# One PSUM bank for cosine and sine products, and the cosine product in three one-pass products

## The chip, the cores and the metric

The kernel runs on one core of one Trainium2 chip. The metric is device time in microseconds, the median of the runs. The core's engines are TensorE (PE in the profile, its weight loads PEld), VectorE (DVE), ScalarE (ACT), GpSimd (POOL) and SyncE (SP), which issues the transfers. Each works through its own queue in order and waits for the others by semaphores.

## The reference

An FNet mixing block (the real part of a two-dimensional FFT over sequence and features) feeds two matrix products with a leaky ReLU between them:

```python
def _attn_ref(x):                      # x: (8, 3008, 256) float32
    X = np.fft.fft(x, axis=1)
    X = np.fft.fft(X, axis=2)
    return X.real.astype(np.float32)

def _moe_ref(x, w_in, w_out):          # x: (24064, 256), w_in: (256, 2048), w_out: (2048, 256)
    h = x @ w_in
    g = np.maximum(0.01 * h, h)
    return (g @ w_out).astype(np.float32)
```

Everything is float32.

## The kernel before, in words

The FFT over the sequence is done with folds on VectorE and small products on TensorE. Its result lies in SBUF as `mix_sb[0]` (cosine part, `mixc` in the profile) and `mix_sb[1]` (sine part, `mixs`). The FFT over the features is multiplied into `w_in` ahead of time: `wf[:, 0]` and `wf[:, 1]` are the folded input weights for the two parts. With c the product for the cosine part and s the one for the sine part, c + s is the hidden value at one sequence frequency and c - s the one at the mirrored frequency.

After a start of 504 frequencies that is done otherwise, the rest is cut into 23 chunks of at most 504 columns (class `Chunk`, t = 0 to 22). A chunk has 16 **steps**, one for each block of 128 hidden units (f = 0 to 15). A step of chunk t does this, with the line numbers of the profile of before:

- ScalarE writes into the cosine bank the share of the middle feature frequency, `nb_sb` times a column of weights `wn` (`seed`, L1248, two steps ahead: `seed_next`).
- TensorE adds the cosine product to the cosine bank and writes the sine product into the sine bank (`up`, L1253). There are two banks of each, `cos_psa`, `cos_psb`, `sin_psa`, `sin_psb`, used in turn.
- ScalarE copies the cosine bank to SBUF (`cos_sb`, L1259).
- VectorE writes copy + sine bank and copy - sine bank into `block_sb` (`hidden`, L1266, two instructions).
- One step later ScalarE applies the leaky ReLU in place there (L1529).

`block_sb` is a pool of 28 slots of four hidden blocks each; a chunk's 16 values lie there, and sums of them. The output product is done in the manner of a fast matrix product: 28 sums of values (`sum`, L1283; table `SUMS`, those in `ON_GPSIMD` on GpSimd, the others on VectorE), 26 products of four matrix products each (`product`, L1304; 104 in a chunk, into the banks `sum_psa` to `sum_psc`), copies of some results by ScalarE (L1321), and sums of the results on VectorE (`make`, L1350). The weights of these products stream from DRAM into a ring of nine places (`wr`, SP's L783), six ahead.

The transform of the following columns goes on meanwhile in small pieces: folds on VectorE (L1094, L1096, L1118), helper copies on ScalarE (L1113, L1121, L870), products on TensorE (L838).

**What sets the order.** `rest()` makes a list of events, each with a time in steps, sorts it and emits the instructions in that order. Step f of chunk t stands at 16t + 1.20 + f, the products of chunk t from 16t + 18.1 at 6.5 in a step, the sums at the times in `SUMS_AT`. So TensorE's queue holds, for each step, cosine, sine and six or seven output products. VectorE's pieces of the transform and its sums of results are given out at two places of each step (`some(1)` at whole numbers, `some(0)` at the end of a step's event). All of one engine's instructions then run in that order.

Of the kernel before, what the change touches and what calls it, by code (L numbers as in the profile page):

```python
# [9 lines left out]
F32 = mybir.dt.float32  # L10
I32 = mybir.dt.int32
# [115 lines left out]
ON_GPSIMD = (1, 2, 4, 5, 7, 10, 11, 13, 14, 15, 18, 19, 20, 22, 23, 24, 26, 27)  # L127
# [200 lines left out]
def tile_fnet_leaky_relu(  # L328
# [21 lines left out]

    block_sb = const.tile([P, SLOTS * SS], F32, name="block")
    part_sb = const.tile([P, PARTS * NMAX], F32, name="part")
    cos_sb = const.tile([P, 2, 2 * NMAX], F32, name="cos")
    small_sb = const.tile([P, NF + 10], F32, name="small")
# [15 lines left out]
    def ring(tag):  # L370
# [5 lines left out]
    assert weights_at - 4 * P >= lay_out(block_sb, 0, (("g", 5, 2 * WN), ("win", 4, WN), ("power", 2, WN), ("raw", 1, 2 * WN), ("o", 2, 2 * WN),  # L376
                                               ("e", 2, 2 * WN), ("s", 4, 2 * WN)))
    head_at = {
        "part": [part_sb, lay_out(part_sb, 0, (("cos", 3, WN), ("out", 2, 2 * WN), ("we", 1, WN), ("nyq", 1, UW[0]))), PARTS * NMAX],
        "cos": [cos_sb.rearrange("p a n -> p (a n)"), 0, 4 * NMAX],  # L380
    }
# [8 lines left out]
    rings["ev"] = [0, [ev_sb, in_head(KC)]]  # L390
    rings["e0"] = [0, [e0_sb, in_head(384)]]
# [193 lines left out]
    wf = const.tile([P, 2, F], F32, name="wf")  # L585
# [3 lines left out]
    wt = block_sb[:, weights_at:].rearrange("p (i g n) -> p i g n", g=4, n=P)  # L589
    w_dram = dram.tile([8 + len(W_SUMS), P, 4 * P], F32, name="w_dram")  # L590
    feat_sb = block_sb[:, weights_at - 4 * P : weights_at].rearrange("p (a n) -> p a n", a=2)
    nyx = in_parts(4 * NT * B, 2, 2, NT, B)[0:LOADED]
    nyz = in_parts(16 * B, 16, B)[0:LOADED]
    nyf = in_parts(8 * FI * B, 2, 2, 2 * FI, B, where="cos")[0:LOADED]
    angle, inf, lrelu, touched = (small_sb[:, NF + at : NF + at + n] for at, n in ((0, 6), (6, 2), (8, 1), (9, 1)))
# [118 lines left out]
    def fold_w_in(f0, n, made, tag="up", pieces=1, queue=nc.sync, sums=None):  # L714
# [13 lines left out]
        for odd, at in places:  # L728
            w = m if odd else n
            for i in (1, 0):  # L730
                rows = slice(half, P) if i != odd else slice(0, half)
                nc.scalar.copy(wf[rows, i, f0 + at : f0 + at + w], banks[odd, at][rows, 0:w])
                if i == 1 and odd == 0:
                    spread_wn(f0, n, queue)

    def spread_wn(f0, n, queue):

        for q in range(f0 // P, (f0 + n) // P):
            queue.dma_start(wn[:, q : q + 1], wf[P // 2 : P // 2 + 1, 1, q * P : (q + 1) * P])
# [58 lines left out]

    reach = [w % 4 for w in range(8)]
# [4 lines left out]
    stream = Stream()  # L804
# [219 lines left out]
    def raised(j, f):  # L1024
# [3 lines left out]
        for blk in range(2):  # L1028
            for h in range(2):
                nc.tensor.matmul(pt[blk][:, h * n : (h + 1) * n], lhsT=wf[:, blk, fs[h] * P : (fs[h] + 1) * P],  # L1030
# [3 lines left out]
    def activate(j, f, later=None):  # L1034
# [19 lines left out]
        if later is not None:  # L1054
            later.append([g])
# [101 lines left out]
    class Slots:  # L1157
# [32 lines left out]
        def rows(self, r, g, n):  # L1190
            steps = {y - x for x, y in zip(r, r[1:])}
            return [self.row(a, g, n) for a in ([r] if len(steps) == 1 else [r[0:2], r[2:4]])]

# [25 lines left out]
    class Chunk:  # L1219
# [18 lines left out]
        def half(self, f):  # L1238

            return home[0] if self is every[0] and f < EARLY else f % 2  # L1240

        def touch(self, f, since):

            nc.tensor.matmul(cos_ps[self.half(f)][:, since : self.w], lhsT=wf[:, 0, 0:P], rhs=mix_sb[0][:, since : self.w],
                             start=False, stop=True, skip_group_check=True)

        def seed(self, f):
            nc.scalar.activation(cos_ps[self.half(f)][:, 0 : self.w], nb_sb[:, self.lo : self.lo + self.w], ACT.Copy, scale=wn[:, f : f + 1])  # L1248
# [530 lines left out]
```

## Time and profile before

| | |
|---|---|
| Runs, median (lowest to highest) | 1809.29 us (1809.08 to 1809.91), three runs |
| Profiled execution, first to last instruction | 1807.9 us |
| TensorE busy | 1801.6 us |
| VectorE busy | 1535.2 us |
| ScalarE busy | 1042.9 us |
| GpSimd busy | 1034.3 us |
| Granted TensorE clock, mean | 1.000 |

No own time of the profiled execution is given beside its span; 1807.9 us is the span, and the median of the runs is 1.4 us above it.

A row of a group reads: line, engine, operation, written tile, read tiles, shapes, count, then busy time in us and the mean duration of one in ns, then the idle time of the engine just before these instructions and what ended it. A row of the timeline reads: start, time covered, engine, line, operation, count, and in brackets idle time of the engine before it with what ended it. A row of waits reads: who waited for whom, total us, how often, the longest. A row of windows reads: the stretch, its length, and then for each engine busy time and, in brackets, its number of instructions (PE, PEld, DVE, ACT, POOL), the granted clock, the share of the DMA engines and GB/s. TensorE's records overlap: an fp32 product shows as two weight loads and two matmul records, each of which lasts about 0.17 us beyond the start of the next one.

### The profile page before, as it was taken

To read this page: it belongs to the slowest core of one execution; us is meant where nothing else is said; L and a number is where in the kernel's file an instruction comes from. 1 tells how busy PE (TensorE), PEld (TensorE's weight loads), DVE (VectorE), ACT (ScalarE), POOL (GpSimd) and SP (SyncE) were. 2 spreads that over 40 slices of the span, in tenths; PEclk is the share of its full clock that TensorE was granted. 3 is DMA by queue.
4 is the path that set the end of the run, shared out by engine and by line. 5 is a ranking of instruction groups with operands and counts; after the bars stand their busy time and mean duration, and the time that the engine had idled before them with its cause. 6 is when DMAs were issued, how large, how long until landed. Compare 5 with 4: busy or idle time off the path is not lost.

```text
span 1807.9 us, 22509 instructions
## 1 busy us (share of the span) xinstructions
PE 1801.6 (100%) x7232; PEld 1336.7 (74%) x7232; DVE 1535.2 (85%) x2614; ACT 1042.9 (58%) x1785; POOL 1034.3 (57%) x443
## 2 busy tenths in 40 slices
PE   9999999999999999999999999999999999999999
PEld 7867777777777777777777777777777777777778
DVE  8899888788798987999869988789887897876868
ACT  4687556665556655665556655566555665555540
POOL 2236666766565665755656656556566565566730
PEclk9999999999999999999999999999999999999999
DMA  7365345433363333624435234443333533323324
GB/s 253 104 216 177 95 136 171 149 118 103 117 199 115 122 117 116 223 79 137 135 128 182 90 119 133 150 160 114 128 132 125 173 124 115 122 90 109 121 90 153
DMA packets 144115, 245.88 MB, mean 136 GB/s; under 512 B 17392, under 2 KB 53872, under 8 KB 144000
## 3 DMA queue, kind: packets, MB, share of 16 engines
q1 hardware_dynamic: 143856, 244.46, 41.5%
q8 instruction: 58, 0.95, 0.2%
q14 instruction: 57, 0.47, 0.1%
q10 hardware_dynamic: 144, 0.00, 0.0%
HBM read 212.86 MB, written 31.54 MB: 135 GB/s over the span
## 4 chain that ended last, share of the span: by engine, by line
PE 97%; DVE 1%; ACT 1%; DMA 0%; issue 0%; DVEq 0%
PE sum_psc L1304 21%; PE sum_psa L1304 17%; PE sum_psb L1304 17%; PE sin_psb L1253 9%; PE cos_psb L1253 9%; PE cos_psa L1253 8%; PE sin_psa L1253 8%; PE dft_ps L838 3%; PE sum_psa L1075 1%; PE sum_psc L1075 1%; PE sum_psb L1075 1%; PE dft_ps L1075 1%; PE cos_psa L1030 0%; PE sin_psa L1030 0%; DMA block<-in_w_in_dram 0%; PE sin_psb L1030 0%
## 5 line engine op out<-in xcount | busy, mean ns | idle before, releaser
L1283 POOL TENSOR_TENSOR block<-block 128x1008 f32<-128x1008 f32 (+1 forms) x396 | 995.5, 2525 | 620.2 <-DVE xt L1096 164.1
L1304 PE MATMUL sum_psc<-block,wr 128*128 128x252 f32 (+1 forms) x1832 | 426.0, 375 | 0.8 <-DMA wr<-w_dram 0.8
L1283 DVE TENSOR_TENSOR block<-block 128x1008 f32<-128x1008 f32 (+1 forms) x248 | 417.2, 1687 | 1.5 <-POOL block L1283 1.4
L1304 PEld LDWEIGHTS sum_psc<-block,wr 128*128 128x128 f32 x1832 | 347.8, 190 | 94.7 <-issue 60.4
L1529 ACT ACTIVATE block<-block 128x504 f32<-128x504 f32 (+3 forms) x510 | 393.2, 798 | 4.5 <-DVE block L1266 4.4
L1266 DVE TENSOR_TENSOR block<-cos,sin_psa 128x504 f32<-128x504 f32 (+1 forms) x356 | 224.3, 671 | 150.1 <-PE sin_psa L1253 149.5
L1304 PE MATMUL sum_psb<-block,wr 128*128 128x252 f32 (+1 forms) x1472 | 347.4, 376 | 0.0
L1304 PE MATMUL sum_psa<-block,wr 128*128 128x252 f32 (+1 forms) x1480 | 344.6, 376 | 0.0
L1304 PEld LDWEIGHTS sum_psb<-block,wr 128*128 128x128 f32 x1472 | 277.5, 190 | 85.2 <-issue 56.2
L1304 PEld LDWEIGHTS sum_psa<-block,wr 128*128 128x128 f32 x1480 | 280.5, 190 | 68.2 <-issue 41.0
L1266 DVE TENSOR_TENSOR block<-cos,sin_psb 128x504 f32<-128x504 f32 (+1 forms) x380 | 239.3, 671 | 93.5 <-PE sin_psb L1253 91.9
L1259 ACT COPY cos<-cos_psb 128x504 f32<-128x504 f32 (+1 forms) x190 | 109.5, 576 | 243.5 <-PE cos_psb L1253 243.5
L1259 ACT COPY cos<-cos_psa 128x504 f32<-128x504 f32 (+1 forms) x178 | 102.7, 577 | 244.4 <-PE cos_psa L1253 244.4
L1253 PE MATMUL sin_psb<-mixs,wf 128*128 128x504 f32 (+1 forms) x380 | 191.2, 585 | 0.6 <-DVE block L1266 0.6
L1253 PE MATMUL cos_psb<-mixc,wf 128*128 128x504 f32 (+1 forms) x380 | 191.0, 585 | 0.0
L1350 DVE TENSOR_TENSOR part<-part 128x252 f32<-128x252 f32 (+1 forms) x342 | 183.1, 573 | 1.3
L1253 PE MATMUL cos_psa<-mixc,wf 128*128 128x504 f32 (+1 forms) x356 | 178.9, 584 | 0.0
L1253 PE MATMUL sin_psa<-mixs,wf 128*128 128x504 f32 (+1 forms) x356 | 178.9, 584 | 0.0
L1253 PEld LDWEIGHTS sin_psb<-mixs,wf 128*128 128x128 f32 x380 | 72.1, 190 | 88.9 <-issue 72.9
L1248 ACT ACTIVATE cos_psb<-nb,small 128x504 f32<-128x504 f32 (+1 forms) x190 | 129.8, 683 | 6.2
L1253 PEld LDWEIGHTS sin_psa<-mixs,wf 128*128 128x128 f32 x356 | 67.7, 190 | 82.0 <-issue 67.3
L1248 ACT ACTIVATE cos_psa<-nb,small 128x504 f32<-128x504 f32 (+1 forms) x178 | 121.6, 683 | 5.8
(213 smaller groups left out, 1329.6 us busy)
## 6 DMA issues: line engine op xcount, KB each, us to landing
wr<-w_dram SPq DMA_DIRECT2D x575, 256.0 KB, 3.5
xt<-in_x_dram SPq DMA_DIRECT2D x28, 1024.0 KB, 7.1
out_dram<-part SPq DMA_DIRECT2D x120, 126.0 KB, 1.8
out_dram<-part SPq DMA_DIRECT2D x64, 124.5 KB, 2.0
tabe<-in_seq_tab_dram SPq DMA_DIRECT2D x29, 190.0 KB, 4.0
w_dram<-block SPq DMA_DIRECT2D x18, 256.0 KB, 7.1
block<-in_w_in_dram SPq DMA_DIRECT2D x8, 512.0 KB, 4.4
block<-in_w_out_dram SPq DMA_DIRECT2D x8, 512.0 KB, 5.1
```

Of the source, the lines that this page charges most:

```text
L838: nc.tensor.matmul(o, lhsT=still, rhs=moving, start=(i == 0), stop=(i == 3), skip_group_check=True)
L1075: nc.tensor.matmul(sums[j][d][:, r * n : (r + 1) * n], lhsT=wo[:, fs[h] // 4, fs[h] % 4, d], rhs=a[r][h], start=(f == 0 and r == 0 and h = ...
L1248: nc.scalar.activation(cos_ps[self.half(f)][:, 0 : self.w], nb_sb[:, self.lo : self.lo + self.w], ACT.Copy, scale=wn[:, f : f + 1])
L1253: nc.tensor.matmul(bank[:, 0 : self.w], lhsT=wf[:, i, f * P : (f + 1) * P], rhs=mix_sb[i][:, self.lo : self.lo + self.w], start=(i == 1), ...
L1259: nc.scalar.copy(copy, cos[:, 0 : self.w])
L1266: nc.vector.tensor_tensor(block.row(to, g, self.n), x, y, op=op)
L1283: ins = (engine or nc.gpsimd).tensor_tensor(self.value(16 + i), xa, ya, op=ALU.add if sign > 0 else ALU.subtract)
L1304: nc.tensor.matmul(to, lhsT=stream.weight(self.t, q, g), rhs=self.value(v)[:, g], start=(first and at == 0), stop=(last and g == 3), skip_ ...
L1350: ins = nc.vector.tensor_tensor(part_of[self.copy[v]][:, 0:n], xa, ya, op=ALU.add if sign > 0 else ALU.subtract)
L1529: nc.scalar.activation(to, to, ACT.Lrelu)
```

## The change

For a chunk from the third on (t >= 2, `PARTED_FROM`), the cosine product is no longer one fp32 product but three products of operands of type float32r. Weights and moving columns are each split in a high part (scaled by 1 - 2^-13 and rounded to the type) and a low part; a third part, `both`, combines the two. TensorE multiplies high by high and low by low into the bank, ScalarE rescales the bank in place by 1 + 2^-12, and TensorE adds the product of the two `both` parts. The weights' parts are made once (`parted_weights`, on ScalarE and GpSimd in the steps 18 to 26) and kept in DRAM; SP loads one block of 128 x 384 words in each step into one of four places, which before held the cosine weights (`Parted`). The columns' parts are made once for each chunk (`parts`, one instruction each on ScalarE, VectorE and GpSimd).

In all chunks the sine product now goes into the same bank as the cosine product, after ScalarE has copied the cosine product times 2 to SBUF. The bank then holds c + s, and VectorE writes only 2c - (c + s) = c - s. The leaky ReLU reads c + s from the bank and writes it to `block_sb`, and does c - s in place. The four banks are used in turn, one for each step.

A step's event becomes three: `up` at 1.20 + f, `up_third` 0.45 later (third product, ScalarE's copy, the load of the weights four steps ahead, the second leaky ReLU of the step before) and `up_sine` 0.85 later (sine product, VectorE's difference). In the last step of all they stand 0.1 and 0.2 later.

Besides: three sums of each chunk (numbers 5, 14 and 20 of `SUMS`) move from GpSimd to VectorE; `block_sb` has 27 slots and not 28, the weight ring 8 places and not 9, `part_sb` 17 tiles and not 24.

**TensorE, a step of a middle chunk.** Before (`cos` and `sin` banks, `wf` the weights; the L1304 rows are the output products):

```order
L1304 MATMUL sum_psc<-block,wr 128x252 x6
L1253 MATMUL cos_psb<-mixc,wf 128x498
L1253 MATMUL sin_psb<-mixs,wf 128x498
L1304 MATMUL sum_psc<-block,wr 128x252
L1304 MATMUL sum_psa<-block,wr 128x252 x4
```

Of the change (L1320 a one-pass product with the parts `mixed` and `parted`, L1324 the sine product, L1401 the output products):

```order
L1320 MATMUL cos_psb<-mixed_963,parted_1264 128x504 x2
L1401 MATMUL sum_psb<-block,wr 128x249 x3
L1320 MATMUL cos_psb<-mixed_963,parted_1264 128x504
L1401 MATMUL sum_psb<-block,wr 128x249 x2
L1324 MATMUL cos_psb<-mixs,wf_sin 128x504
L1401 MATMUL sum_psb<-block,wr 128x249
L1320 MATMUL sin_psb<-mixed_963,parted_1370 128x504 x2
L1401 MATMUL sum_psb<-block,wr 128x249 x2
L1401 MATMUL sum_psc<-block,wr 128x249
L1320 MATMUL sin_psb<-mixed_963,parted_1370 128x504
L1401 MATMUL sum_psc<-block,wr 128x249 x3
L1324 MATMUL sin_psb<-mixs,wf_sin 128x504
```

Cosine and sine stood side by side; now five or six output products (and in some steps products of the transform) lie between the first pair and the sine of the same bank.

**ScalarE, the same place, with the semaphores that each instruction waits for.** Before (L1259 copy of the cosine bank, L1248 seed, L1113 a copy for the transform, L1529 leaky ReLU, L1321 copy of a result):

```order
L1259 COPY cos<-cos_psa 128x504 [waits PE_49]
L1248 ACTIVATE cos_psa<-nb,small 128x504 [waits Activation_49]
L1529 ACTIVATE block<-block 128x2x252 [waits DVE_49] x2
L1259 COPY cos<-cos_psb 128x504 [waits PE_49]
L1248 ACTIVATE cos_psb<-nb,small 128x504 [waits Activation_49]
L1529 ACTIVATE block<-block 128x4x252 [waits DVE_49,Pool_49]
```

Of the change (L1345 rescale in place, L1588 leaky ReLU, from the bank for c + s and in place for c - s, L1334 seed, L1353 doubled copy, L1314 `high` part of a later chunk's columns):

```order
L1345 ACTIVATE sin_psb<-sin_psb 128x498 [waits PE_49]
L1588 ACTIVATE block<-cos_psb 128x2x249 [waits DVE_49]
L1334 ACTIVATE sin_psa<-nb,small 128x498 [waits Activation_49]
L1353 ACTIVATE cos<-sin_psb 128x498 [waits PE_49]
L1588 ACTIVATE block<-block 128x2x249
L1418 COPY part<-sum_psb 128x252 [waits PE_49]
L1345 ACTIVATE cos_psa<-cos_psa 128x498 [waits PE_49]
L1588 ACTIVATE block<-sin_psb 128x2x249 [waits DVE_49]
L1334 ACTIVATE cos_psb<-nb,small 128x498 [waits Activation_49]
L1314 ACTIVATE mixed_963<-mixc 128x504
L1353 ACTIVATE cos<-cos_psa 128x498 [waits PE_49]
L1588 ACTIVATE block<-block 128x2x249
```

The leaky ReLU of c + s, which reads a PSUM bank, waits for VectorE: for the difference of the same bank, which reads that bank too. It stands between the rescale and the doubled copy of the next step. The one in place, which follows, has no wait of its own left. In 48 steps the first one also waits for GpSimd.

**VectorE, some steps of a chunk's second half.** Before (L1266 sum and difference, L1283 sums of values, L1350 sums of results, L1094 and L1096 the transform):

```order
L1266 TENSOR_TENSOR block<-cos,sin_psa 128x2x249 x2
L1350 TENSOR_TENSOR part<-part,sum_psc 128x252
L1283 TENSOR_TENSOR block<-block 128x1008
L1266 TENSOR_TENSOR block<-cos,sin_psb 128x2x249 x2
L1350 TENSOR_TENSOR part<-part,sum_psa 128x252 x2
L1350 TENSOR_TENSOR part<-part 128x252 x2
L1266 TENSOR_TENSOR block<-cos,sin_psa 128x2x249 x2
L1094 TENSOR_TENSOR half<-half,dft_ps 128x2x94
L1094 TENSOR_TENSOR half<-half,dft_ps 128x188
L1096 TENSOR_TENSOR mixc<-half 128x376 x2
L1266 TENSOR_TENSOR block<-cos,sin_psb 128x2x249 x2
```

Of the change (L1363 the difference, L1380 sums of values, L1447 sums of results, L1159 and L1161 the transform):

```order
L1363 TENSOR_TENSOR block<-cos,sin_psa 128x2x249
L1447 TENSOR_TENSOR part<-part,sum_psc 128x252
L1363 TENSOR_TENSOR block<-cos,cos_psb 128x2x249
L1380 TENSOR_TENSOR block<-block 128x1008
L1447 TENSOR_TENSOR part<-part,sum_psa 128x252 x2
L1159 TENSOR_TENSOR half<-half,dft_ps 128x2x94
L1159 TENSOR_TENSOR half<-half,dft_ps 128x188
L1447 TENSOR_TENSOR part<-part 128x252 x2
L1161 TENSOR_TENSOR mixc<-half 128x376 x2
L1363 TENSOR_TENSOR block<-cos,sin_psb 128x2x249
```

Each step has one instruction of this kind where it had two, and the work between two of them falls otherwise: here a sum of values, three kinds of the transform and four sums of results lie in one step.

The core of the diff:

```diff
-ON_GPSIMD = (1, 2, 4, 5, 7, 10, 11, 13, 14, 15, 18, 19, 20, 22, 23, 24, 26, 27)
+ON_GPSIMD = (1, 2, 4, 7, 10, 11, 13, 15, 18, 19, 22, 23, 24, 26, 27)
-SLOTS, RS, SS, PARTS = 28, 252, 1008, 24
-RING, RING_AHEAD = 9, 6
+SLOTS, RS, SS, PARTS = 27, 252, 1008, 17
+RING, RING_AHEAD = 8, 6
+PARTED_FROM = 2
+UPPER, SHIFT = 1.0 - 2.0**-13, 2.0**12
+PARTS_AT, PARTED_WEIGHTS_AT = -2.7, 18
+UP_THIRD, UP_SINE = 0.45, 0.85
...
+        def parts(self):
+            m = mixed[self.t % 2].rearrange("p (i n) -> p i n", i=3)
+            high, low, both = (m[:, i, 0 : self.w] for i in range(3))
+            src = mix_sb[0][:, self.lo : self.lo + self.w]
+            nc.scalar.activation(high, src, ACT.Copy, scale=UPPER)
+            nc.vector.scalar_tensor_tensor(both, in0=high, scalar=1.0 + 1.0 / SHIFT, in1=src, op0=ALU.mult, op1=ALU.subtract)
+            nc.gpsimd.tensor_tensor(low, src, high, op=ALU.subtract)
...
         def up(self, f):
-            cos, sin = cos_ps[self.half(f)], sin_ps[self.half(f)]
-            for i, bank in enumerate((cos, sin)):
-                nc.tensor.matmul(bank[:, 0 : self.w], lhsT=wf[:, i, f * P : (f + 1) * P], rhs=mix_sb[i][:, self.lo : self.lo + self.w],
-                                 start=(i == 1), stop=True, skip_group_check=True)
+            if self.t < PARTED_FROM:
+                self.product_of_rows(f, 0)
+                return
+            bank = self.bank_of(f)[:, 0 : self.w]
+            self.product_of_parts(f, 0)
+            self.product_of_parts(f, 1)
+            nc.scalar.activation(bank, bank, ACT.Copy, scale=1.0 + 1.0 / SHIFT)
+
+        def up_third(self, f):
+            if self.t >= PARTED_FROM:
+                self.product_of_parts(f, 2)
+                parted.load(NF * (self.t - PARTED_FROM) + f + F // WN)
...
+            nc.scalar.activation(cos_sb[:, f % 2, 0 : self.w], self.bank_of(f)[:, 0 : self.w], ACT.Copy, scale=2.0)
+
+        def up_sine(self, f):
+            self.product_of_rows(f, 1)
...
+            plus, minus = (block.row(i, g, self.n) for i in (r[0:2], r[2:4]))
+            both = self.bank_of(f)[:, 0 : self.w].rearrange("p (j n) -> p j n", j=2)
+            nc.vector.tensor_tensor(minus, cos_sb[:, f % 2, 0 : self.w].rearrange("p (j n) -> p j n", j=2), both, op=ALU.subtract)
+            return [(plus, both), (minus, minus)]
...
+            elif kind == 5:
+                every[t].up_third(i)
+                activate_some()
+                folds.emit_copies()
...
+                some(0)
+            elif kind == 6:
+                waiting.append(every[t].up_sine(i))
             else:
...
-                part = every[t]
-                made = part.up(i)
+                every[t].up(i)
+                activate_some(1)
                 seed_next(16 * t + i)
```

`product_of_parts` and `product_of_rows` are one `nc.tensor.matmul` each; `activate_some(1)` emits the leaky ReLU of c + s of the step before, `activate_some()` the rest.

More of the change, by code (lines that the diff above doesn't have):

```diff
@@ L797, in used, with parted_weights, here, __init__ @@
             self.load_to(self.of[t, q] + 1 + RING_AHEAD)
+    mixed = []
+    def parted_weights(i):
+        if not mixed:
+            mixed.extend(late.tile([P, 6 * NMAX], F32R, name=f"mixed{j}", tag=f"mixed{j}") for j in range(2))
+            nc.scalar.activation(wn_less, wn, ACT.Copy, scale=1.0 / (1.0 + 1.0 / SHIFT))
+        def here(i):
+            m = mixed[i % 2][:, 0 : 6 * P].rearrange("p (f i n) -> p f i n", f=2, i=3)
+            return m, *(m[:, :, j] for j in range(3))
+        if i > 0:
+            m, high, low, both = here(i - 1)
+            nc.scalar.activation(low, both, ACT.Copy, scale=SHIFT)
+            nc.gpsimd.tensor_tensor(both, low, high, op=ALU.subtract)
+            f = 2 * (i - 1)
+            nc.sync.dma_start(parted_dram[f : f + 2].rearrange("f p n -> p f n"), m.bitcast(F32).rearrange("p f i n -> p f (i n)"))
+        if i < NF // 2:
+            m, high, low, both = here(i)
+            src = wf(0, 2 * i * P, 2 * P).rearrange("p (f n) -> p f n", f=2)
+            nc.scalar.activation(high, src, ACT.Copy, scale=UPPER)
+            wait_for_gate(nc.gpsimd.tensor_tensor(both, src, high, op=ALU.subtract))
+    class Parted:
+        def __init__(self):
+            self.places, self.count = [], NF * (len(chunk) - PARTED_FROM)
+        def load(self, i):
+            n = F // WN
+            if i >= self.count:
+                return
+            if i < n:
+                self.places.append(late.tile([P, 3 * P], F32R, name=f"parted{i}", tag=f"wf{i}"))
+            nc.sync.dma_start(self.places[i % n].bitcast(F32), parted_dram[i % NF])
+        def weight(self, i, part):
+            return self.places[i % (F // WN)][:, part * P : (part + 1) * P]
     reach = [w % 4 for w in range(8)]
@@ L1458, in seed @@
                 t, f = ups[at]
-                widest = max(part.w for part in every[: t or 1])
-                if f < 2 and every[t].w > widest:
-                    every[t].touch(f, widest)
+                if at == 1:
+                    every[t].touch(f, 4 * KB[0])
                 every[t].seed(f)
@@ L1481, in rest, with activate_some @@
         todo, until, empty = work(), 0, -1
+        def activate_some(count=None):
+            for of in waiting:
+                for to, x in of[:count]:
+                    nc.scalar.activation(to, x, ACT.Lrelu)
+                del of[:count]
+            waiting[:] = [of for of in waiting if of]
         def go_on(step):
@@ L1519, in rest @@
                         some(pool)
+            elif kind == 4:
+                every[t].parts()
+            elif kind == 5:
+                every[t].up_third(i)
+                activate_some()
+                folds.emit_copies()
+                for call in behind[1:]:
+                    call()
+                behind[:] = [None]
+                some(0)
+            elif kind == 6:
+                waiting.append(every[t].up_sine(i))
             else:
```

95 lines of the change are left out of this document (54 added, 41 removed).

## The prediction

> **What bounds the kernel now.** I read the page's busy table and the chain that ended last first, then the waits, then one step in the timeline.
>
> ```profile
> span 1807.9 us, 22509 instructions
> ...
> PE 1801.6 (100%) x7232; PEld 1336.7 (74%) x7232; DVE 1535.2 (85%) x2614; ACT 1042.9 (58%) x1785; POOL 1034.3 (57%) x443
> ...
> PE 97%; DVE 1%; ACT 1%; DMA 0%; issue 0%; DVEq 0%
> ```
>
> TensorE is busy for 1801.6 of 1807.9 us and is 97% of the chain. Work taken off it shortens the kernel, but only if nothing makes it wait. The waits say why nothing does now:
>
> ```profile
> ACT cos L1259 <- PE cos_psa L1253: 244.4, 167, 2.4
> ACT cos L1259 <- PE cos_psb L1253: 243.5, 181, 2.0
> DVE block L1266 <- PE sin_psa L1253: 149.5, 93, 4.0
> ...
> DVE block L1266 <- PE sin_psb L1253: 91.9, 64, 3.8
> ...
> ACT block L1529 <- DVE block L1266: 4.4, 6, 1.2
> ```
>
> ```profile
> PE sin_psb L1253 <- DVE block L1266: 0.6, 2, 0.3
> ```
>
> ScalarE stands ready for 348 of the 368 cosine copies and waits for TensorE. VectorE stood waiting for the sine bank only 93+64 = 157 times of 368: in most steps it comes to its two sums late. Nobody minds, because ScalarE's leaky ReLU, which reads them, comes much later (6 waits, 4.4 us), and TensorE needs neither before the bank's next turn (0.6 us). A step:
>
> ```profile
> 825.35 1.00 PE L1253 MATMUL cos_psa<-mixc,wf 128*128 128x498 f32 x2
> 826.19 1.00 PE L1253 MATMUL sin_psa<-mixs,wf 128*128 128x498 f32 x2
> 826.39 0.57 ACT L1259 COPY cos<-cos_psa 128x498 f32<-128x498 f32 x1 [1.88 <-PE cos_psa L1253]
> 827.00 0.68 ACT L1248 ACTIVATE cos_psa<-nb,small 128x498 f32<-128x498 f32 x1
> 827.02 2.71 PE L1304 MATMUL sum_psc<-block,wr 128*128 128x252 f32 x12
> 828.28 1.25 DVE L1266 TENSOR_TENSOR block<-cos,sin_psa 128x498 f32<-128x498 f32 x2
> 829.57 1.00 PE L1253 MATMUL cos_psb<-mixc,wf 128*128 128x498 f32 x2
> ```
>
> Each fp32 product is two records. From start to start an upward product takes 826.19 - 825.35 = 0.84 us, a downward one 0.424 us (twelve records in 2.71 us, of which 0.17 is the last one's tail), the step 4.22 us. The sine result was there at 827.19 and VectorE took it at 828.28, 1.09 us late.
>
> **A. The matmuls.** In 336 steps (chunks 2 to 22, 16 each) one cosine product of 0.84 us becomes three of one pass. The trace has none. Nearest rows:
>
> ```profile
> L1253 PE MATMUL cos_psb<-mixc,wf 128*128 128x504 f32 x252 | 127.1, 586 | 0.0
> L1304 PE MATMUL sum_psc<-block,wr 128*128 128x252 f32 x1200 | 279.6, 376 | 0.0
> ```
>
> A one-pass product of 504 columns costs 0.42 us at most (one record of this width) and 0.21 at least (the record of half the width). I take 0.21: the two weight loads of an fp32 product show its weights split in two, and the moving operand must then be split as well, which makes a record two passes. So 336 x (0.84 - 3 x 0.21) = **-70 us**; at 0.42 it would be +141. The Trainium skill, FP8 and Floating Point Precision (TensorE Precision Notes), counts four passes for true FP32, by which a pass is 0.84/4 = 0.21 us and the sum the same; no run here shows a single pass yet.
>
> **B. The new round trips.** Before, TensorE ran cosine and sine one after the other into two banks. Now one bank takes pair, ScalarE's rescale, third product, ScalarE's doubled copy, sine, each waiting for the one ahead, and between rescale and copy ScalarE's queue holds the leaky ReLU of the sum and a seed. Time from the pair's start, with ScalarE free:
>
> ```profile
> 131.10 0.58 ACT L1259 COPY cos<-cos_psb 128x504 f32<-128x504 f32 x1 [0.67 <-PE cos_psb L1253]
> 131.58 0.69 ACT L1248 ACTIVATE cos_psa<-nb,small 128x504 f32<-128x504 f32 x1
> ...
> 132.20 0.68 ACT L1248 ACTIVATE cos_psb<-nb,small 128x504 f32<-128x504 f32 x1
> ```
>
> ```profile
> 1015.99 1.13 ACT L1529 ACTIVATE block<-block 128x504 f32<-128x504 f32 x2
> ```
>
> ```profile
> 98.37 1.26 DVE L1266 TENSOR_TENSOR block<-cos,sin_psb 128x504 f32<-128x504 f32 x2
> ...
> 99.68 1.11 PE L1253 MATMUL sin_psb<-mixs,wf 128*128 128x504 f32 x2 [0.27 <-DVE block L1266]
> ```
>
> Pair 0.42, tail 0.17 and 0.04 until ScalarE starts (826.39 after 826.35): 0.63. Rescale to next start 0.48 (131.10 to 131.58), ReLU 0.5, seed 0.62 (to 132.20), copy 0.58. Then 0.05 to TensorE (VectorE ends at 99.63, TensorE starts at 99.68) and 0.10 for a weight load that no longer hides (1.11 for the pair of records, not 1.01). Sum **2.96 us**. TensorE itself needs, by the order, pair, three downward products, third, two more: 0.42 + 3 x 0.424 + 0.21 + 2 x 0.424 = 2.75 us. So it waits 0.21 us. In the steps with three more (3.17 us) or with transform products between, it doesn't. Of 336 steps 149 are of the first kind: **+31 us** (0 if ScalarE's steps are 0.05 shorter each, 52 if 0.05 longer). The third product needs the rescale at 0.63 + 0.6 + 0.15 = 1.38 and is reached at 1.69: nothing.
>
> **C. Guests in ScalarE's queue.** In 21 steps two copies of sums stand ahead of the doubled copy, in 20 the new `high` part:
>
> ```profile
> 823.89 0.62 ACT L1321 COPY part<-sum_psb 128x252 f32<-128x252 f32 x2
> ```
>
> Each adds 0.5 to 0.6 us, 0.21 of which half the steps have to spare: 41 steps x some 0.4, **+15 us** (8 to 25).
>
> **D. VectorE on the path.** The order of the change shows that the leaky ReLU of the sum waits for VectorE's difference of the same bank, in every step. It stands ahead of seed and doubled copy, so VectorE's lateness now reaches TensorE's sine. The Trainium skill, PSUM — Partial Sum Buffer (PSUM bank collisions raise a hardware error), says that two engines must not touch one bank at once, two readers included, which speaks against putting both readers on one bank; no wait of the kernel before shows such a pair, and without it D would be 0 and the sum -21 us.
>
> The difference can start 0.2 us before the next pair and takes 0.67; the ReLU would start at 0.63 + 0.48 = 1.11. VectorE may thus be 0.6 us late; before, the ReLU came at 829.57 + 1.04 + 0.61 + 0.61 = 831.83, so 3.4 us (831.83 - 827.19 - 1.25). Is it lighter loaded?
>
> ```profile
> 150.00:950.00 800.00, 800.00 (x3214) 591.16 (x3213) 684.19 (x1166) 472.00 (x812) 497.04 (x200) 1.00 0.41 133
> ```
>
> ```profile
> L1283 DVE TENSOR_TENSOR block<-block 128x1008 f32<-128x1008 f32 x150 | 274.8, 1832 | 1.4 <-POOL block L1283 1.4
> L1266 DVE TENSOR_TENSOR block<-cos,sin_psb 128x504 f32<-128x504 f32 x252 | 159.2, 672 | 67.5 <-PE sin_psb L1253 66.2 <-ACT cos L1259 0.8
> L1350 DVE TENSOR_TENSOR part<-part 128x252 f32<-128x252 f32 x225 | 120.3, 572 | 0.8
> L1096 DVE TENSOR_TENSOR mixc<-half 128x376 f32<-128x376 f32 x14 | 26.8, 1954 | 0.2
> ```
>
> ```profile
> 148.71 1.00 PE L1253 MATMUL cos_psa<-mixc,wf 128*128 128x498 f32 x2
> ...
> 1753.19 1.00 PE L1253 MATMUL cos_psb<-mixc,wf 128*128 128x498 f32 x2
> ```
>
> Before: chunk 1's first step starts at 148.71 us, the last chunk's last at 1753.19, 351 steps later: 4.57 us a step, of which VectorE works 684/800, 3.90 us. The change takes one sum (159.2/252 = 0.63 us) and adds 3 of GpSimd's per chunk, 3 x 1.83/16 = 0.34, and a part, 0.04: 3.65 us in a step of 4.57 - 0.21 = 4.36, 84% as against 85%. Not lighter, and in bursts. Adding VectorE's rows between two differences by their busy time per instruction, and lowering all by 5% so that the same count gives 3.90 before, three pairs of steps in a chunk exceed 2 x 4.36 us: the last with the next first 10.1, the seventh with the eighth 9.8, the thirteenth with the fourteenth 11.2. Less 8.7 and the 0.6 of slack: 0.8 + 0.5 + 1.9 = 3.2 us a chunk, 67 us in 21. GpSimd's part of the competition shrinks, since it does 15 sums a chunk, not 18, and B gives VectorE time: I take **+40 us** (20 to 85).
>
> **E. The rest.** In chunks 0 and 1 two cosine products are followed at once by their sine: 0.21 + 0.58 + 0.15, together **+3 us** (0 to 10). The weights' parts add 336 loads of 192 KB, 66 MB:
>
> ```profile
> q1 hardware_dynamic: 143856, 244.46, 41.5%
> ...
> wr<-w_dram SPq DMA_DIRECT2D x575, 256.0 KB, 3.5
> ```
>
> They are issued three and a half steps (15 us) ahead and land in about 3.5 us at 41.5 to 53% busy queues: nothing; a load that came late would cost its lateness once. ScalarE gains 336 rescales of 0.58 us, 58% to some 69% busy, no bound by itself.
>
> **Sum:** -70 + 31 + 15 + 40 + 3 = +19 on 1807.9, so 1827 us of span; the runs' median lies 1.4 us above the profiled span: **1828 us, 1% slower**.
>
> **Rivals.** *The gain stays* (30%). All waits together need to stay under 70/336 = 0.21 us a step. For it: VectorE waited 157 times, so many differences will be on time, and B vanishes if each ScalarE step is 0.05 us shorter. Against: its bursts are in the order. With B 10, C 10, D 20, E 3 it is -27: 1782 us. *They cancel* (7%): 1806 to 1813. *GpSimd joins in* (7%): in 48 steps that ReLU also waits for a GpSimd sum that still reads the slot it writes, now that there are 27 slots; at half of a GpSimd sum, 1.25 us, that is +60: 1888 us.
>
> ```profile
> L1283 POOL TENSOR_TENSOR block<-block 128x1008 f32<-128x1008 f32 x270 | 682.5, 2538 | 407.6 <-DVE xt L1096 115.9 <-PE sum_psb L1304 101.4 <-DVE block L1283 61.6
> ```
>
> *The products are not what they are called* (3%): 0.42 us each, +141; TensorE then reaches its sines after 2.96 us and the steps grow to 5 us, so B and D go: 1955 us. My forecast has 53%.
>
> **How the numbers follow.** Faster by over 0.2% (3.6 us, about what a measurement can tell from nothing) 0.30, within it 0.07, slower 0.63. My forecast's own range, from B, C, D at their ends without all at once, is 1813 to 1870. The range for 8 in 10 takes in the better part of the first rival: 1776 to 1870.
>
> **What would show it.** TensorE's busy time near 1735 us with idle time near 90, put down to the doubled copy as releaser of the sine (its first record 0.1 us longer); one-pass records 0.21 us apart; ScalarE's ReLU of the sum waiting for VectorE's difference, some 50 us in all, in the bursts named. Wrong in A if the records stand 0.42 apart; in B and D if TensorE has under 30 us of idle time; in E if it waits for weights.

## The result, and the profile after

The changed kernel takes 2046.28 us (median of four runs, 2042.60 to 2047.21) against 1809.24 us: 1.131 times as long, with a 95% interval of 1.129 to 1.132. Slower was forecast, but 19 us slower, not 237. From the page of the changed kernel (span; busy time, share and instructions of each engine; shares of the chain that ended last):

```profile
span 2045.3 us, 23322 instructions
...
PE 1834.1 (90%) x7570; PEld 1388.1 (68%) x7570; DVE 1488.0 (73%) x2333; ACT 1196.7 (59%) x2387; POOL 899.3 (44%) x414
...
PE 43%; DVE 32%; ACT 16%; issue 5%; POOL 2%; DMA 1%; DVEq 0%; ACTq 0%
```

TensorE, 97% of the chain before, is now 43% of it. It is idle for 2045.3 - 1834.1 = 211 us, where it was for 6; that is 205 of the 237 us. The other 32 are in its busy time, which was to fall. No other engine is busy for more than 73%. The waits of the changed kernel (who waited for whom: us in total, times, longest):

```profile
ACT block L1588 <- DVE block L1363: 272.4, 170, 4.7
...
DVE xt L1183 <- ACT dft_ps L1186: 88.3, 39, 3.8
PEld sin_psb L1324 <- ACT cos L1353: 84.5, 62, 3.2
PEld cos_psa L1324 <- ACT cos L1353: 82.1, 74, 2.5
PEld cos_psb L1324 <- ACT cos L1353: 80.5, 85, 2.7
...
DVE xt L1159 <- ACT dft_ps L1178: 69.5, 42, 3.1
...
PE sin_psb L1324 <- ACT cos L1353: 61.6, 40, 2.8
...
PE cos_psa L1324 <- ACT cos L1353: 54.8, 44, 2.1
PEld sin_psa L1324 <- ACT cos L1353: 54.6, 40, 3.0
PE cos_psb L1324 <- ACT cos L1353: 49.8, 33, 2.3
...
PE sin_psa L1324 <- ACT cos L1353: 38.9, 39, 2.6
```

L1588 is the leaky ReLU (L1529 before), L1363 the difference, L1353 the doubled copy, L1324 the sine. ScalarE's wait for the difference was 4.4 us in 6 steps; it is 272 us in 170. TensorE's weight loads for the sine then wait for the copy in 62 + 74 + 85 + 40 = 261 steps; in 156 of these (the PE rows: 40 + 44 + 33 + 39) TensorE visibly stands still, for 205 us in all, nearly its whole idle time. Matching the two lists by time, 200 of these 205 us (146 steps) fall in steps whose ReLU had just waited for VectorE. But two rows go the other way: VectorE, too, waits for ScalarE, for copies of the transform (L1186, L1178). One step and a half of the timeline (start, duration, what; in brackets the idle time before it and who ended it):

```profile
1164.40 0.67 DVE L1363 TENSOR_TENSOR block<-cos,sin_psa 128x504 f32<-128x504 f32 x1
...
1165.10 0.59 ACT L1588 ACTIVATE block<-sin_psa 128x504 f32<-128x504 f32 x1 [2.19 <-DVE block L1363]
...
1165.58 0.68 ACT L1334 ACTIVATE cos_psa<-nb,small 128x498 f32<-128x498 f32 x1
1166.18 0.58 ACT L1353 ACTIVATE cos<-cos_psb 128x504 f32<-128x504 f32 x1
...
1166.82 1.11 PE L1324 MATMUL cos_psb<-mixs,wf_sin 128*128 128x504 f32 x2 [2.17 <-ACT cos L1353]
1167.17 0.76 ACT L1186 ACTIVATE dft_ps<-xt,small 95x128 f32<-95x128 f32 x2
...
1167.96 0.60 DVE L1183 SCALAR_TENSOR_TENSOR xt<-xt,small,dft_ps 95x128 f32<-95x128 f32 x2 [2.24 <-ACT dft_ps L1186]
...
1168.48 1.74 DVE L1380 TENSOR_TENSOR block<-block 128x1008 f32<-128x1008 f32 x1
...
1170.14 1.20 DVE L1447 TENSOR_TENSOR part<-part 128x252 f32<-128x252 f32 x3
...
1171.25 0.67 DVE L1363 TENSOR_TENSOR block<-cos,cos_psb 128x504 f32<-128x504 f32 x1
...
1171.96 0.59 ACT L1588 ACTIVATE block<-cos_psb 128x504 f32<-128x504 f32 x1 [2.53 <-DVE block L1363]
```

The difference comes late, so ReLU, seed, copy and sine do. Behind them on ScalarE stands a copy that VectorE waits for: VectorE loses 2.24 us, does its sum and parts, and brings the next difference 6.85 us after the last (1171.25 - 1164.40). Each engine is late because the other was; the experiments take the two causes apart.

### The profile page after: what moved, and what is told of

The parts are those of the page before. It is cut to its first block, busy times and chain, and to the rows that moved or that the text cites. A ratio compares the mean times of both kernels' runs of the same rounds, so it can differ in the third digit from the quotient of the medians.

```text
span 2045.3 us, 23322 instructions
## 1 busy us (share of the span) xinstructions
PE 1834.1 (90%) x7570; PEld 1388.1 (68%) x7570; DVE 1488.0 (73%) x2333; ACT 1196.7 (59%) x2387; POOL 899.3 (44%) x414
## 4 chain that ended last, share of the span: by engine, by line
PE 43%; DVE 32%; ACT 16%; issue 5%; POOL 2%; DMA 1%; DVEq 0%; ACTq 0%
DVE block L1380 11%; PE sum_psc L1401 9%; PE sum_psb L1401 7%; PE sum_psa L1401 7%; DVE part L1447 6%; ACT block L1588 5%; DVE block L1363 5%; DVE xt L1161 4%; PE sin_psb L1324 3%; ACT cos L1353 3%; PE sin_psa L1324 3%; PE cos_psb L1324 2%; PE cos_psa L1324 2%; DVE xt L1159 2%; POOL block L1380 2%
## 5 line engine op out<-in xcount | busy, mean ns | idle before, releaser
L1380 POOL TENSOR_TENSOR block<-block 128x1008 f32<-128x1008 f32 (+1 forms) x330 | 810.2, 2465 | 938.1 <-DVE block L1380 301.9
L1380 DVE TENSOR_TENSOR block<-block 128x1008 f32<-128x1008 f32 (+1 forms) x314 | 588.6, 1883 | 40.0 <-ACT block L1588 16.3
L1401 PE MATMUL sum_psc<-block,wr 128*128 128x252 f32 (+1 forms) x1832 | 463.3, 375 | 0.0
L1401 PEld LDWEIGHTS sum_psc<-block,wr 128*128 128x128 f32 x1832 | 347.6, 190 | 104.2 <-issue 62.6
L1401 PE MATMUL sum_psa<-block,wr 128*128 128x252 f32 (+1 forms) x1480 | 385.4, 380 | 0.0
L1401 PE MATMUL sum_psb<-block,wr 128*128 128x252 f32 (+1 forms) x1472 | 376.1, 376 | 0.0
L1401 PEld LDWEIGHTS sum_psa<-block,wr 128*128 128x128 f32 x1480 | 283.0, 193 | 97.1 <-issue 60.7
L1401 PEld LDWEIGHTS sum_psb<-block,wr 128*128 128x128 f32 x1472 | 279.8, 191 | 79.6 <-issue 45.1
L1588 ACT ACTIVATE block<-block 128x504 f32<-128x504 f32 (+1 forms) x372 | 234.6, 631 | 3.1 <-DVE block L1116 3.1
L1447 DVE TENSOR_TENSOR part<-part 128x252 f32<-128x252 f32 (+1 forms) x342 | 164.3, 512 | 23.8 <-ACT part L1418 22.5
L1324 PE MATMUL sin_psb<-mixs,wf_sin 128*128 128x504 f32 (+1 forms) x190 | 103.0, 624 | 61.7 <-ACT cos L1353 61.6
L1324 PE MATMUL cos_psb<-mixs,wf_sin 128*128 128x504 f32 (+1 forms) x190 | 106.5, 643 | 50.2 <-ACT cos L1353 49.8
L1324 PE MATMUL cos_psa<-mixs,wf_sin 128*128 128x504 f32 (+1 forms) x178 | 99.4, 641 | 54.8 <-ACT cos L1353 54.8
L1324 PE MATMUL sin_psa<-mixs,wf_sin 128*128 128x504 f32 (+1 forms) x178 | 97.7, 632 | 38.9 <-ACT cos L1353 38.9
L1320 PE MATMUL cos_psb<-mixed,parted 128*128 128x504 f32 (+1 forms) x252 | 118.6, 526 | 0.0
L1320 PE MATMUL sin_psb<-mixed,parted 128*128 128x504 f32 (+1 forms) x252 | 117.3, 520 | 0.2 <-ACT sin_psb L1345 0.2
L1320 PE MATMUL sin_psa<-mixed,parted 128*128 128x504 f32 (+1 forms) x252 | 116.8, 518 | 0.0
L1363 DVE TENSOR_TENSOR block<-cos,sin_psa 128x504 f32<-128x504 f32 (+1 forms) x89 | 59.7, 671 | 77.5 <-PE sin_psa L1324 77.5
L1320 PE MATMUL cos_psa<-mixed,parted 128*128 128x504 f32 (+1 forms) x252 | 115.7, 513 | 0.0
L1363 DVE TENSOR_TENSOR block<-cos,cos_psb 128x504 f32<-128x504 f32 (+1 forms) x95 | 63.6, 670 | 67.5 <-PE cos_psb L1324 67.5
L1345 ACT ACTIVATE sin_psa<-sin_psa 128x504 f32<-128x504 f32 (+1 forms) x84 | 48.2, 573 | 109.2 <-PE sin_psa L1320 108.5
L1345 ACT ACTIVATE cos_psb<-cos_psb 128x504 f32<-128x504 f32 (+1 forms) x84 | 48.7, 580 | 106.7 <-PE cos_psb L1320 106.7
```

What stands on the lines that cost most here:

```text
L1320: nc.tensor.matmul(self.bank_of(f)[:, 0 : self.w], lhsT=parted.weight(NF * (self.t - PARTED_FROM) + f, i), rhs=m[:, i, 0 : self.w], start= ...
L1324: nc.tensor.matmul(self.bank_of(f)[:, 0 : self.w], lhsT=wf(i, f * P, P), rhs=mix_sb[i][:, self.lo : self.lo + self.w], start=False, stop=T ...
L1345: nc.scalar.activation(bank, bank, ACT.Copy, scale=1.0 + 1.0 / SHIFT)
L1363: nc.vector.tensor_tensor(minus, cos_sb[:, f % 2, 0 : self.w].rearrange("p (j n) -> p j n", j=2), both, op=ALU.subtract)
L1380: ins = (engine or nc.gpsimd).tensor_tensor(self.value(16 + i), xa, ya, op=ALU.add if sign > 0 else ALU.subtract)
L1401: nc.tensor.matmul(to, lhsT=stream.weight(self.t, q, g), rhs=self.value(v)[:, g], start=(first and at == 0), stop=(last and g == 3), skip_ ...
```

## The experiments

The theories put on record were: (1) VectorE's lateness reaches the sine through the ReLU that waits for the difference; (2) VectorE is too full; (3) the round trip over ScalarE is itself too long; and later (4) VectorE's own waits for ScalarE's copies. Each variant was run once or twice; two runs of one variant lie at most 1.6 us apart, the four of the changed kernel 4.6 us.

### One bank, the products, the sums

> The changed kernel without its one-pass products: all chunks take the fp32 cosine product of chunks 0 and 1, so there is no rescale, no parts and no load of the weights' parts; one bank, the wait for VectorE and the moved sums stay. Theory 1 (the wait for VectorE on the sine's path): the products cost some 50 us more, the stalls stay about as they were less a little for the shorter queue of ScalarE: 2000-2070 us. Theory 3 (rescale and round trip): idle time of TensorE falls under 80 us, time 1850-1920 us.

```diff
-PARTED_FROM = 2
+PARTED_FROM = 23
...
```

2009.33 us, as theory 1 had it. Its busy row and its largest wait (in the changed kernel ScalarE spends some 410 us waiting for the pair ahead of its rescale, which is missing here, so more of the same delay shows at the ReLU):

```profile
PE 1877.5 (94%) x7234; PEld 1344.5 (67%) x7234; DVE 1410.2 (70%) x2312; ACT 1009.5 (50%) x2013; POOL 847.2 (42%) x377
```

```profile
ACT block L1588 <- DVE block L1363: 775.9, 331, 5.5
```

Without one-pass products, rescale and parts the kernel is still 200 us slower than before: 124 us of it are TensorE's idle time (130 instead of 6), 76 its busy time. So the loss comes with the one bank and its single VectorE operation, not with the products; the three moved sums and the smaller buffers were still in this run.

> Only the one-pass products, in another split: high by high, high by low and low by high one after the other into the cosine's own bank, no rescale; the sine in its own bank as before, sum and difference both on VectorE, the sums divided between VectorE and GpSimd as before, 27 slots. By the trace of the changed kernel a one-pass product takes 0.23 us, so a step's TensorE time falls from 4.22 to 4.07 us, 336 x 0.15 = 50 us. Theory 1 and 3: nothing waits, as before: 1755-1775 us. Theory 2 (VectorE too full): VectorE works 3.9 of 4.4 us a step and becomes late often enough to give part of it back: 1775-1815 us. If one-pass products really cost 0.42 us beside fp32 ones, no gain or a loss: 1810-1850 us.

```diff
...
-            self.product_of_parts(f, 0)
-            self.product_of_parts(f, 1)
-            nc.scalar.activation(bank, bank, ACT.Copy, scale=1.0 + 1.0 / SHIFT)
+            for i in range(3):    # high*high, high*low, low*high
+                self.product_of_parts(f, i)
+            self.sine_of(f)       # own bank
...
+            nc.vector.tensor_tensor(plus, x, y, op=ALU.add)
+            nc.vector.tensor_tensor(minus, x, y, op=ALU.subtract)
...
```

1758.56 us, in the range of theories 1 and 3, and 0.972 of the time before (0.969 to 0.975): faster than both kernels. Its busy row, and TensorE's timeline:

```profile
PE 1749.8 (100%) x7568; PEld 1396.5 (80%) x7568; DVE 1587.1 (90%) x2614; ACT 1070.6 (61%) x1886; POOL 1083.4 (62%) x472
```

```profile
1001.01 1.00 PE L1305 MATMUL sin_psa<-mixs,wf_sin 128*128 128x498 f32 x2
1001.84 2.29 PE L1404 MATMUL sum_psc<-block,wr 128*128 128x252 f32 x10
1003.97 0.59 PE L1404 MATMUL sum_psa<-block,wr 128*128 128x252 f32 x2
1004.21 1.03 PE L1320 MATMUL cos_psb<-mixed,parted 128*128 128x498 f32 x3
1005.07 1.00 PE L1305 MATMUL sin_psb<-mixs,wf_sin 128*128 128x498 f32 x2
```

A step takes 1005.07 - 1001.01 = 4.06 us instead of 4.22. TensorE's busy time falls by 1801.6 - 1749.8 = 52 us, 0.154 a step, so three one-pass products take 0.84 - 0.154 = 0.69 us, 0.23 each. With 90% VectorE is busier than in any one-bank kernel, and TensorE still stands idle for only 6 us, as before.

> The changed kernel with the other split of the one-pass products: high by high, high by low and low by high in a row into the bank, no rescale and no third part; one bank, doubled copy, only the difference on VectorE, the moved sums. Theory 1 (the wait for VectorE is the cost of the one bank, with or without rescale): 50 us less TensorE work than with fp32 products, so 1950-2010 us, with 120 us or more of idle time in front of the sine. Theory 3 (the rescale's round trip is the cost): 1760-1850 us.

The same products, without rescale, in one bank (of the diff above only the loop of three products in place of pair and rescale): 1997.10 us, as theory 1 had it. The bank form, with the three sums that go with it, is worth 239 us.

> The changed kernel with the three sums of each chunk back on GpSimd (18 there, 10 on VectorE, as before). It takes 69 sums of 1.88 us, some 130 us, off VectorE. Theory 1 (a wait for VectorE on the sine's path): VectorE is less late, the wait stays where it is: 30 to 90 us less than 2046, so 1955-2015 us. Theory 2 (VectorE too full in bursts): most of the stalls go, time under 1930 us. Theory 3 (the round trip itself): no change, 2030-2050 us.

```diff
-ON_GPSIMD = (1, 2, 4, 7, 10, 11, 13, 15, 18, 19, 22, 23, 24, 26, 27)
+ON_GPSIMD = (1, 2, 4, 5, 7, 10, 11, 13, 14, 15, 18, 19, 20, 22, 23, 24, 26, 27)
```

2046.00 us: no change, which only theory 3 had forecast. But VectorE's lateness didn't shrink either: ScalarE's ReLU waited for it for 273.6 us (272.4 before). VectorE's busy time fell from 1488 to 1436 us only, and its waits for ScalarE grew (L1186 from 88.3 to 102.9, L1178 from 69.5 to 93.4 us), so the run doesn't speak for theory 3. Theory 1's 30 to 90 us were missed all the same.

> The kernel with three products in a row and two banks, with the three sums of each chunk on VectorE as in the change. VectorE was busy for 1587 of 1756 us there; 69 sums of 1.88 us more are 130 us, so 98% if they take what such sums took. If VectorE's load counts: 1775-1830 us. If the sums run faster there because GpSimd is out of VectorE's way more: 1755-1765 us.

Where nothing holds VectorE up, the same three sums cost 1769.96 - 1758.56 = 11.4 us; it is then busy for 1656 of 1768 us, 94%. The time lies between the two forecasts. This is also the closest partner of the one-bank run above: with the same products and the same sums the bank form alone (one bank, doubled copy, single difference, the order that goes with it) costs 1997.10 - 1769.96 = 227 us.

### Where the ReLU stands

> The changed kernel with one edit: ScalarE's leaky ReLU of cosine plus sine is written behind the doubled copy of the next step instead of ahead of it. Theory 1 (a wait for VectorE put on the sine's path): the 211 us that TensorE stood still came from that ReLU waiting for VectorE's difference in front of the copy that the sine needs; with the copy ahead of it TensorE's idle time falls under 70 us and the time to 1840-1900 us. Theory 2 (VectorE is too full in bursts, wherever ScalarE waits for it): the wait only moves to the next rescale; idle time stays above 120 us, time 1950-2050 us. Theory 3 (the round trip pair, rescale, third, copy, sine is itself too long): the chain gets 0.5 us shorter without the ReLU, idle time falls by 50 us or so, time near 1990 us.

```diff
                 every[t].up(i)
-                activate_some(1)
```

> The ReLU of cosine plus sine behind the next step's doubled copy, as in the run before of this kind, and with what that run had left wrong put in order: there the first 12 steps' seeds and one sum of each chunk came ahead of the ReLU that they need, so that part of the output was of unfinished values. Now the ReLU keeps its old place in those 12 steps, and that sum (of values 5 and 13) is due at 17.70 instead of 17.24. Theory 1: the time stays at 1895-1930 us, with some 90 us of idle time in front of the third product, as the late difference now reaches the rescale of the step after. If the wrong order had made the gain, 1990-2046 us.

1913.00 us for the first, 1916.89 for the second, which is the one to go by. 129 us come back, within theory 1's second range, although ScalarE's ReLU still waits 276 us for the difference (272 in the changed kernel): it no longer does so ahead of the copy. The sine's wait is nearly gone (12 us), and 93 us of TensorE's idle time stand ahead of the third product (L1320) instead, which waits for the rescale (L1345) behind the ReLU. The largest row of each:

```profile
PE cos_psa L1320 <- ACT cos_psa L1345: 36.2, 19, 3.2
...
PE sin_psb L1324 <- ACT cos L1353: 8.0, 7, 2.1
```

The first range (under 70 us idle) was too hopeful.

> The changed kernel with the two readers of the bank in the other order: ScalarE's leaky ReLU of cosine plus sine is written ahead of VectorE's difference of the same bank, which then waits for ScalarE; nothing else is moved. Theory 1 (VectorE's lateness reaches the sine through that ReLU): the ReLU now waits only for the sine; VectorE's difference comes 1 to 1.5 us later, and what is left is the ReLU of the difference, which stands behind the doubled copy: TensorE's idle time falls from 211 to under 60 us, 1800-1870 us. Theory 3 (the round trip over rescale, ReLU, seed and copy is itself too long): the ReLU stands where it stood, idle time stays above 120 us, 1940-2046 us.

```diff
...
-            nc.vector.tensor_tensor(minus, cos_sb[:, f % 2, 0 : self.w].rearrange("p (j n) -> p j n", j=2), both, op=ALU.subtract)
...
+                if of and len(of[0]) == 3:     # behind the ReLU of c + s
+                    to, x, y = of[0]
+                    nc.vector.tensor_tensor(to, x, y, op=ALU.subtract)
...
```

1905.16 us, between the two forecasts; TensorE's visible waits are 25 us at the sine and 50 at the third product. The waits show what took over:

```profile
DVE block L1591 <- ACT block L1587: 257.8, 175, 3.6
ACT block L1587 <- DVE block L1591: 236.4, 157, 3.8
```

VectorE now waits for the ReLU of the sum, and ScalarE, one ReLU on, for the difference, ahead of the next rescale.

> The kernel with the ReLU of cosine plus sine ahead of the difference, and now the ReLU of the difference too taken from the path: it is written behind the rescale of the step after the next instead of behind the next doubled copy (and the sum of values 14 and 2 is due at 18.21 instead of 17.74). Theory 1 (what was left, 79 us of idle time in front of sine and third product, came from that ReLU waiting for the late difference ahead of the next rescale): idle time under 35 us, 1820-1870 us. If VectorE is then full (it was busy 80%), or other waits take its place: 1880-1905 us.

```diff
...
-                activate_some()
...
+                if len(waiting) > 1:           # behind up() and its rescale
+                    (to, x), = waiting.pop(0)
+                    nc.scalar.activation(to, x, ACT.Lrelu)
...
```

1938.31 us: worse than the run before it, and above both ranges. VectorE is off the path (8% of the chain), but the moved ReLU now stands between rescale and copy:

```profile
PE 63%; ACT 24%; DVE 8%; issue 4%; POOL 1%; DMA 1%; SPq 0%; DVEq 0%; ACTq 0%
```

```profile
1000.70 0.80 PE L1320 MATMUL sin_psb<-mixed,parted 128*128 128x504 f32 x2
...
1004.25 1.11 PE L1324 MATMUL sin_psb<-mixs,wf_sin 128*128 128x504 f32 x2
```

From pair to sine 3.55 us pass on ScalarE's chain, where TensorE itself, in the shorter steps, needs some 3.0 (pair 0.64, six records 1.09, third 0.41, four records 0.85, by the starts in its timeline). 149 such steps (the count of the prediction) by 0.55 us are 82; the sine waits 90, in 178 steps. So the round trip (theory 3) does cost what is added to it. In the changed kernel the chain is shorter by that one ReLU, some 0.5 us, and just fits.

### What makes VectorE late

> The changed kernel with VectorE's 13 sums of values left out in chunks 2 to 22 (the values that they would make are stale, so the output is not the reference's); the order of all else, the one bank, the rescale and ScalarE's queue stay. It prices the round trip pair, rescale, ReLU, seed, copy, sine with a VectorE that is seldom late. Theory 1 (the stalls are VectorE's unevenness, step by step): TensorE's idle time falls from 211 to under 60 us, time 1790-1850 us. Theory 3 (the round trip itself): idle time over 130 us, time over 1930 us. In between: VectorE's waits for ScalarE's own copies, which stand behind that ReLU, hold the difference up too.

```diff
+            if engine is None or self.t < PARTED_FROM:
+                ins = (engine or nc.gpsimd).tensor_tensor(...)
...
```

> The changed kernel with VectorE's instructions of the transform reading the copies' source instead of ScalarE's copies (the turned ones so lose their factor, and the one-pass part of x its rounding: the output isn't the reference's); ScalarE still makes the copies, so both queues hold the same work, but VectorE no longer waits for them (88 + 70 + 46 us before). Theory 4 (VectorE's waits for copies that stand behind the ReLU that waits for VectorE): some 70 of the 211 us of idle time go, time 1935-1985 us. If VectorE's own work alone makes it late: 2020-2050 us.

```diff
-            self.tensor_tensor(to, x, copy, op)
+            ... nc.vector.tensor_tensor(to, x, y, op=op)
...
+                tmp = [y, y]
...
-  scalar_tensor_tensor(both, in0=high, ...
+  scalar_tensor_tensor(both, in0=src, ...
```

> Both left out together: VectorE's 13 sums a chunk and its waits for ScalarE's copies. What is left is the round trip pair, rescale, ReLU, seed, copy, sine, for which the prediction had 31 us, and 15 for the guests in ScalarE's queue. If VectorE's lateness is the whole rest: idle time 20-55 us, time 1800-1850 us. If the round trip costs more than was counted: idle time over 70 us, over 1870 us.

| kernel | time, us | TensorE waiting for the copy, us | VectorE busy |
|---|---|---|---|
| changed | 2046.28 | 205 | 73% |
| no wait for copies | 1992.44 | 149 | 79% |
| no VectorE sums | 1914.69 | 99 | 51% |
| neither | 1875.30 | 64 | 56% |

Without the sums VectorE is half idle, and 99 us stay: the time lies between the ranges of theories 1 and 3. It then waits more for ScalarE's copies, not less:

```profile
DVE xt L1159 <- ACT dft_ps L1178: 156.4, 72, 3.4
...
ACT block L1589 <- DVE block L1363: 141.9, 128, 4.7
DVE xt L1183 <- ACT dft_ps L1186: 128.6, 39, 4.1
```

Taking those waits away brings TensorE 56 us with the sums and 35 without, less than the 70 forecast, and the time is just above the range; VectorE's instructions that read the source instead also took longer (busy 1580.8 us, not 1488.0), so the price of the waits is rather more. What remains in "neither" is above its range too: 56 of the 64 us still follow a ReLU that waited for VectorE, since VectorE still waits for ScalarE's copies of results (L1421, 53.7 us) and has its other work. 9 us follow no such wait. So the two causes, VectorE's sums and its waits for ScalarE's copies, explain 141 of the 205; most of the rest is VectorE's lateness too, but which piece of its work brings it wasn't taken apart.

### A sine in one pass too

> The kernel with three products in a row and two banks (1758.56 us), with the sine in three one-pass products as well from chunk 3 on: its x and weights split in the same way, 256 KB of parts loaded a step instead of 128. TensorE saves another 0.15 us in 320 steps, 48 us, if one-pass products cost 0.23 us: 1705-1725 us. VectorE was busy for 1587 of 1756 us and comes near 93%: if its lateness reaches TensorE, or six in a row save less, 1725-1760 us.

> Six one-pass products a step with the sine's parts made 3.2 steps later, behind the last write of their source (in the run before of this kind they were made ahead of it, from unfinished values). TensorE's work is 29 us less than with three (1720.7 against 1749.8 us busy), VectorE's share 93%: 1735-1765 us if VectorE's lateness keeps taking the gain; 1705-1725 us if the early parts had held it up.

1752.78 us, from unfinished values and in the second range: TensorE's busy time fell by 29 us, not 48, at a granted clock of 0.994. Then 1780.43 in order, above its range and 22 us more than with three products. The sine waits for GpSimd's part:

```profile
PE sin_psa L1311 <- POOL sine_mixed L1331: 49.7, 20, 3.9
```

The source is written until shortly before the chunk begins, so the parts are late by 2.5 us in each of 20 chunks. With TensorE's work at 1721 us this version wants an earlier transform, which was not tried.

## Why the prediction was wrong

**A, the matmuls, right, a little too large.** 0.23 us each, not 0.21: -52 us, not -70. The rival with 0.42 falls. In the changed kernel this gain can't be read from TensorE's busy time, which rose by 32.5 us instead of falling to 1735: some 84 us offset it. Three entries, all estimates, make up most of them. A sine that has waited takes 1.11 us instead of 1.00 (261 steps by 0.1, 26 us); B had counted this 0.10. An output product's record lasts 0.38 us where the next one starts after 0.21, so each time TensorE runs dry, 0.17 us more count as busy (156 times, 26 us). The granted clock, 1.00 before, averages 0.987, which is 24 us of 1834. Some 8 us are left and were not settled. So a stalled step costs more than the idle time that it shows.

**B, the round trip, right.** By both the waits that follow no late ReLU (5 us) and the run with one ReLU more in the chain, it is worth no more than the 31 us forecast. From the pair's shown start to the rescale some 0.83 us pass, not 0.63 (1000.70 to 1001.53 with both ReLUs moved), but TensorE's own part is longer by as much (3.0 us, not 2.75).

**C, the guests, were taken for their time on ScalarE only.** That time is within the same 5 us. That VectorE also waits for such copies, and that they stand behind the ReLU that waits for VectorE, was in the order and was not followed.

**D, VectorE on the path, is the step that failed.** The place, the ReLU of the sum behind the difference, was right; the price was 200 us, not 40 (20 to 85). VectorE's work between two differences is 3.72 us a step from chunk 2 on, close to the 3.65 worked out. But this was compared with TensorE's step over pairs, and only three pairs of a chunk were found too long. Two things were wrong with that. First, with the ReLU ahead of the copy no step can lend another its spare time: the next difference waits for the next sine, which waits behind this difference. Take the 335 steps from one difference to the next, from chunk 2 on, against 4.42 us, the mean of the same steps in two banks (1480.0 us in all). The 88 steps in which VectorE worked without a pause exceed it by 77 us together. Second, VectorE was taken to be late by its work alone: the 109 steps in which it waited for ScalarE exceed it by 131 us; the other 138 add 47. The two runs that take one of these away each (106 and 56 us less waiting of TensorE) bear out both. The sign that the prediction named for D, ScalarE's ReLU waiting some 50 us for the difference, came with 272. How little VectorE's average share says is seen in the runs: 51% busy and 105 us slower than before; 90% busy in two banks and 51 us faster.

**E, right:** 336 more loads landed in 2.4 us and TensorE waited for none. The rival with GpSimd falls (ScalarE's ReLU waits for it nowhere in the list). The rival that the gain stays needed under 0.21 us of waits a step; they were 0.6.

The Trainium skill, PSUM — Partial Sum Buffer (PSUM bank collisions raise a hardware error), says that two engines must not touch one bank at once. The traces agree as far as they go: the two readers of one bank wait for each other in whichever order they are written, ScalarE for VectorE 272.4 us in the changed kernel, VectorE for ScalarE 257.8 us with the ReLU first.

## What to carry to other kernels

Before putting a producer's and a consumer's engine on one short buffer, write out the loop that closes (here difference, ReLU, copy, sine, next difference) and price it step by step, each by its own length and not by the mean: spare time is lent only where there is a buffer to hold it. Follow each in-order queue in both directions, since an engine that is waited for may itself be waiting behind the waiter. The gain of the faster products was real and could be had alone, by leaving the two banks as they were (1758.56 us, with a split that needs no rescale).

## What was not expected of the hardware

A one-pass record that stands beside fp32 ones costs 0.23 us for 498 to 504 columns, though its own row in the timeline shows 0.57 where it is alone: its start is shown with its weight load, 0.03 us after the start of the output product ahead of it, where two output products stand 0.21 us apart. So only whole steps can be priced.

The granted clock fell in most kernels where TensorE stops and starts. In the middle of the run (1000 us of the changed kernel, then of the one with fp32 products in one bank; span, busy times of PE, PEld, DVE, ACT and POOL, PEclk, DMA share, GB/s):

```profile
300.00:1300.00 1000.00, 885.21 (x3666) 672.15 (x3665) 724.85 (x1120) 600.97 (x1209) 462.91 (x195) 0.99 0.49 154
```

```profile
300.00:1300.00 1000.00, 931.54 (x3551) 660.98 (x3550) 695.74 (x1130) 506.86 (x1026) 448.68 (x186) 0.97 0.38 120
```

It is 1.00 before and in two banks. Over the whole run it is 0.987 with 211 us of idle time and 0.977 with 130, but 1.000 with 104 where both ReLUs are moved: the sum of idle time doesn't set it. The trace shows that the clock doesn't sink a little; it halves for single stretches of 3.41 us, which in a run lie whole multiples of that length apart. Two such stretches of the changed kernel, one after the other (columns as above):

```profile
595.55:598.96 3.41, 1.14 (x6) 0.70 (x5) 3.41 (x4) 1.90 (x4) 2.31 (x1) 1.00 0.63 164
598.96:602.38 3.42, 3.42 (x7) 2.08 (x8) 3.42 (x5) 0.78 (x2) 1.14 (x1) 0.50 0.70 236
```

Behind the first 160 us this happens 12 times in the changed kernel, each time right after a stretch in which TensorE was busy for only 24 to 42% of the time, and 24 times with the fp32 products in one bank, after 23 to 44%. Where both ReLUs are moved, TensorE's longest pause in that part is 1.07 us (2.82 in the changed kernel), no 3.41 us are under 68% busy, and the clock never falls. So in these runs a fall goes with a long pause in one place, not with the sum of idle time; the exact limit isn't shown (one stretch with 39% was followed by none).
